# Decayed states in buffers of their own, and half of each row transfer asked for from ScalarE

## The chip, the cores and the metric

The kernel runs on one core of a Trainium2 chip. The core has five engines with an instruction queue each: TensorE (PE), VectorE (DVE), ScalarE (ACT), GpSimd (POOL) and SyncE (SP). Every queue is worked off in order; between engines, semaphores say when something is done. Data moves between the chip's memory and the core's buffers by DMA transfers, which an engine asks for with an instruction of its queue. The metric is the time of one execution on the device in microseconds (us); shorter is better. A change of less than about 1% is called no change here.

## What is computed

Stage 1 is a recurrent (mLSTM) layer over 4 batches, 8 heads, 768 steps and head dimension 40, stage 2 a mixture of 16 experts (4 groups of 4) over its 3072 output rows. Cut to what matters:

```python
for t in range(S):                                   # S = 768, per batch and head
    m_new = np.maximum(f_gate[:, :, t] + m, i_gate[:, :, t])
    f_stab, i_stab = np.exp(f_gate[:, :, t] + m - m_new), np.exp(i_gate[:, :, t] - m_new)
    C = f_stab * C + i_stab * outer(v_t, k_t)        # 40x40 state of each head
    n = f_stab * n + i_stab * k_t
    y[:, :, t] = sigmoid(o_gate[:, :, t]) * (C @ q_t) / max(|n . q_t|, 1)
# stage 2: x = y as [3072, 320]
g_idx = argmax(x @ w_group);  e_idx = argmax(x @ w_expert[g_idx])
out[row] = g_w * e_w * (relu(x[row] @ w1[g, e]) @ w2[g, e])   # w1 320x1024, w2 1024x320
```

## The kernel before

Stage 1 doesn't step through t. It cuts the 768 steps into 12 chunks of 64 and works on two batches at a time, so there are 24 units of work, called pairs here: pair u is chunk c = u // 2 of the batches 2p and 2p+1 with p = u % 2. Inside a chunk everything is a masked matrix product; from chunk to chunk a state `Cst[p]` (128x328, two of them, one for each p) is carried. The state of pair u is read and written again by pair u+2.

`unit(u)` issues the work of one pair. Up to pair 21 what it writes is the order on every engine; from pair 22 on a scheduler decides. In the order of the code, with the names that the rows show (`dst<-src`):

- SP asks for the rows of pair u+3: `load_qk` (L160, queries and keys, two transfers) and, further down, `load_nt` (L170, keys, values and gates, two transfers). There are four buffers of each.
- ACT: `gate_o`, the output gate's tanh (L165).
- PE: `carried(u)` (L239, `Y<-C,qk`): the queries against the state that was carried in; `state(u)` (L256, `Y<-nt,kw`): the chunk's own contribution to the state. Both write into parts of one tile, `Y`.
- POOL: `decayed(u)` (L263, `C<-C,decs`): the state times the chunk's decay, in place.
- DVE: `carried2(u)` (L245, `num<-Y,eacol`), then `state2(u)` (L270, `C<-C,Y`): adds the contribution. PE's `carried(u+1)` writes `Y` again, so it waits until `state2(u)` has read it.
- PE: `values(u)` (L281, `V<-nt,pt`), `scores(u+1)` (L214, `X<-qk`), one filler matmul `busy` (L141) and `decay(u+2)` (L180, L181, `aw`), which ACT turns into `ab` by 8 exponentials (L184).
- DVE: `norm(u)` (L291), `masked(u+1)` (L220, `pt<-X,ab`).
- POOL: `keyw(u+1)` (L227, `kw<-nt,ab`): the keys that `state(u+1)` reads; three buffers in turn.
- `turn(u-1)`: ACT copies, SP writes the pair's rows out (L323, `x_d<-x`), PE transposes them (L317, `tp`), ACT copies again (L333).
- DVE: denominators (`norm1`, L299 to L301) and `rows(u)` (L306, `xn`); POOL: `rows2(u)` (L311, `x<-xn,den`).
- POOL, from pair 6 on: `put_id` (L496, L497), which writes row numbers of the expert lists into the table `itab` in the chip's memory by an indirect DMA.

Every fourth pair, routing work of four earlier pairs is put between (`lg`, L349 to L450, on PE, DVE and ACT), and its weights `cb` are written behind the rows by SP (L452). From pair 12 on, weights of the first experts are asked for by SP (L608) and split into two parts by ACT (L650) and DVE (L652). Stage 2 starts by gathering expert rows: `ix<-itab`, `xg<-x_d,ix` (L590, POOL), a transposition `tpm` (L317, PE), and from there the expert matmuls (L767, L805 to L807).

Of the kernel before, what the change touches and what calls it, by code (L numbers as in the profile page):

```python
# [7 lines left out]
F32 = mybir.dt.float32  # L8
# [4 lines left out]
ALU = mybir.AluOpType  # L13
# [5 lines left out]
P = 128  # L19
B, H, S, D = 4, 8, 768, 40  # L20
L = 64
NP = B // 2
# [3 lines left out]
DM = H * D  # L26
# [9 lines left out]
D1 = D + 1  # L36
R4 = 4 * D1
NQK = 4
QR = 48
KR = 104  # L40
WIDE = 16
NAT = 976
K0, O0 = DM + H, 2 * DM + H
# [22 lines left out]
def bc(ap, shape):  # L66
    return ap.broadcast_to(list(shape))
# [3 lines left out]
def lstm_moe(ctx: ExitStack, tc: tile.TileContext, gates, qkT, nat, wcat, w1, w2, cst, out):  # L71
    nc = tc.nc
# [36 lines left out]
    def att_pool(name, bufs, **kw):  # L109
        return att.enter_context(tc.tile_pool(name=name, bufs=bufs, side="right", **kw))  # L110

    ap_ = att_pool("att", 1)
# [8 lines left out]
    mask_b = ap_.tile([P, L], BF16, name="mask_b")  # L121
    decs = ap_.tile([P, NCH, B * 4], F32, name="decs")
    Cst = [ap_.tile([P, 2, R4], F32, name=f"C{i}") for i in range(NP)]
    kws = [ap_.tile([P, DM + 24], F32, name=f"kw{i}") for i in range(3)]
    bcol = ap_.tile([P, NU, H], F32, name="bcol")
    eacol = ap_.tile([P, NU, H], F32, name="eacol")
    wk = att_pool("wk", 2)
# [9 lines left out]
    def busy(n):  # L137
        if n:
            t = ps_a.tile([P, 512], F32, name="busy", tag="aw", bufs=2)
        for _ in range(n):  # L140
            mm(t, ones_b, bc(ones_b.unsqueeze(1), (P, 4, P)), start=True, stop=True)  # L141
# [15 lines left out]
    def load_qk(u):  # L157
        qk = qkp[u % NQK]
        for r in range(2):
            nc.sync.dma_start(qk[64 * r:64 * r + QR, 4 * P * r:4 * P * r + 8 * P], qkT[u, r].rearrange("d i h t -> d (i h t)"))  # L160
        st_.setdefault(u, {})["qk"] = qk

    def gate_o(u):
# [3 lines left out]
    def load_nt(u):  # L167
        nt = ntp[u % NQK]
        for a in range(2):
            nc.sync.dma_start(nt[halves(a), K0 * a:K0 * a + NAT], nat[u, halves(a)])  # L170
        st_.setdefault(u, {})["nt"] = nt

    def halves(b):
        return slice(L * b, L * b + L)
# [42 lines left out]
    def masked(u):  # L217
        t = st_[u]
        pt = t["pt"] = wk.tile([P, 2, 4 * L], F32, name="pt")
        nc.vector.tensor_tensor(pt, X.rearrange("p r k t -> p r (k t)"), t["ab"].rearrange("p (r i) t -> p r (i t)", r=2),  # L220
                                op=ALU.mult)

    def keyw(u):
        t = st_[u]
        if u // NP < NCH - 1:
            kw = t["kw"] = kws[u % 3]
            nc.gpsimd.tensor_tensor(kw[:, 0:DM].rearrange("p (h d) -> p h d", d=D),  # L227
                                    t["nt"][:, K0:K0 + DM].rearrange("p (h d) -> p h d", d=D),
                                    bc(t["ab"][:, :, L - 1:L], (P, H, D)), op=ALU.mult)
# [29 lines left out]
    def decayed(u):  # L259
        c, p = divmod(u, NP)  # L260
        if 0 < c < NCH - 1:
            cb = Cst[p].rearrange("p a (i e) -> p (a i) e", e=D1)
            nc.gpsimd.tensor_tensor(cb, cb, bc(decs[:, c, p * 8:(p + 1) * 8].unsqueeze(2), (P, 8, D1)), op=ALU.mult)  # L263

    def state2(u):
        c, p = divmod(u, NP)
        if c < NCH - 1:
            st = Y[:, 0, R4:3 * R4].rearrange("p (a x) -> p a x", a=2)
            if c > 0:
                nc.vector.tensor_tensor(Cst[p], Cst[p], st, op=ALU.add)  # L270
            else:
                nc.vector.tensor_copy(Cst[p], st)

# [205 lines left out]
    def first_tokens():  # L479
        none = rt["rows"][0]  # L480
        t = itab[0:NE * NBLK].rearrange("(e n) p o -> e (n p o)", e=NE)
        n = 3 * P * WIDE // 2
        for k in range(2):
            nc.sync.dma_start(t[:, k * n:(k + 1) * n], none[0:NE, 0:n])
        nc.sync.dma_start(itab[NE * NBLK:NE * NBLK + 1].rearrange("a p o -> a (p o)"), none[0:1, 0:P * WIDE])

    def last_rows():
        zero = rt["rows"][1]
        for u in range(NU - 4, NU):
            nc.sync.dma_start(x_d[u * P:(u + 1) * P, :], zero)  # L490
        nc.sync.dma_start(x_d[NTOK:NTOK + 1, :], zero[0:1])
# [340 lines left out]
    def run(stage, u):  # L832
        if 0 <= u < NU:
            stage(u)
# [11 lines left out]

    def unit(u):
        run(load_qk, u + 3)
        if u == 6:
            first_tokens()  # L850
        if u == 9:
            last_rows()
        run(gate_o, u)
        with ExitStack() as st:
            if u == MANUAL:
                st.enter_context(tc.issue_after(rt["lg", u - 3].ins))
            run(carried, u)
        run(state, u)
        run(decayed, u)
        run(carried2, u)  # L860
        parts = ()
        if u % 4 == 1 and 1 < u < NU - 4:
            parts = [lambda f=f: f(u // 4 - 1, 4) for f in (logits_of, logits_at)]
        if u == NU - 4:
            parts = [lambda f=f: f(NG - 2, 3) for f in (logits_of, logits_at)]
        for f in parts[:1]:
            f()
        go_on()
        run(state2, u)
        run(values, u)  # L870
        run(scores, u + 1)
        busy(fill(u))
        run(decay, u + 2)
        run(norm, u)
        run(masked, u + 1)
        for f in parts[1:]:
            f()
        if u > NU - 4:
            run(logits, u - 2)
        if u == 9:  # L880
            chores.append(first_experts())
        if u == 21:
            chores.append(early_counts())
        run(keyw, u + 1)
        run(turn, u - 1)
        run(load_nt, u + 3)
        run(norm1, u)
        run(rows, u)
        run(rows2, u)
        if u == 5:  # L890
            first_rows()
        go_on(3)
        for _ in range(1 if u < 20 else 3):
            put_id()
# [57 lines left out]
    with tc.manual_schedule():  # L952
        nc.sync.dma_start(G[:, :, 0:P], gates[:, :, 0:P])
        nc.scalar.dma_start(cs, cst)
        nc.scalar.dma_start(G[:, :, P:], gates[:, :, P:])
        nc.vector.memset(ones_b, 1.0)
        nc.vector.memset(sep, 0.0)
        nc.scalar.activation(sep, sep, AF.Exp)
        busy(11)
        nc.vector.memset(R_, 1.0)  # L960
        nc.vector.memset(R_.rearrange("h (c t) -> h c t", t=L)[:, :, 0:1], 0.0)
        nc.vector.memset(Dl[:, 0:1], 0.0)
        nc.vector.memset(ohsum[0], 0.0)
        nc.vector.memset(Apc[96:P], 0.0)
        for t in kws:
            nc.gpsimd.memset(t[:, DM:], 0.0)
        for u in range(4):
            q = nc.vector if u % 2 == 0 else nc.gpsimd
            q.memset(qkp[u], 0.0)
            q.memset(ntp[u][0:64, V1:], 0.0)  # L970
            q.memset(ntp[u][64:P, 0:K0], 0.0)
            load_nt(u)
            load_qk(u)
        sel = cs[:, C_SELP:C_SELP + B * H].rearrange("q (a p i) -> q p i a", p=NP, a=2)
        for p in range(NP):
            nc.gpsimd.tensor_copy(selw[:, p].rearrange("q h (b t) -> q h b t", b=2), bc(sel[:, p].unsqueeze(3), (P, H, 2, L)))
        sums.append(gate_sums(0, P))
        nc.gpsimd.tensor_copy(id_b, ident)
        nc.gpsimd.tensor_copy(mask_b, cs[:, C_MASK:C_MASK + L])
        nc.gpsimd.tensor_copy(sel2_b, cs[:, C_SEL2:C_SEL2 + B * 4])  # L980
        nc.gpsimd.tensor_copy(par_b, cs[:, C_PAR:C_PAR + P])
        sum_on(7)
        scores(0)
        decay(0)
        keyw(0)
        sums.append(gate_sums(P, 2 * P))
        sum_on()
        masked(0)
        sum_on()
        decay(1)  # L990
        busy(9)
        state(0)
        values(0)
        scores(1)
        gate_o(0)
        keyw(1)
        norm(0)
        state2(0)
        masked(1)
        decay(2)  # L1000
        norm1(0)
        rows(0)
        rows2(0)
        sum_on()
        nc.gpsimd.iota(tokid[:, :, :, 0], pattern=[[P, NU], [0, WIDE // 2]], base=0, channel_multiplier=1)
        nc.gpsimd.tensor_copy(tokid[:, :, :, 1], bc(cs[:, C_TOK:C_TOK + NU].unsqueeze(2), (P, NU, WIDE // 2)))
        nc.vector.tensor_copy(keyb, cs[:, C_15E:C_15E + NE])
        nc.vector.tensor_copy(lt_b, cs[:, C_LT:C_LT + P])
        nc.vector.tensor_copy(base_b, cs[:, C_BASE:C_BASE + NE])
        nc.sync.dma_start(wc, wcat)  # L1010
        sum_on(7)
        sums.append(gate_sums(2 * P, S))
        for u in range(1, 5):
            unit(u)
            sum_on(2)
        sum_on(9)
# [96 lines left out]
    with tc.For_i(0, nv, 1):  # L1113
# [35 lines left out]
        h = hp.tile([P, NF, P], F32, name="hh")  # L1149
# [99 lines left out]
```

## Time and profile before

| what | value |
|---|---|
| median of 3 runs | 426.79 us (425.06 to 428.4) |
| the profiled execution, its own time | 427.83 us |
| its span in the profile | 426.2 us |
| mean granted TensorE clock | 0.921 |
| busy: PE | 373.5 us (88%) |
| busy: PE's weight loads (PEld) | 332.9 us (78%) |
| busy: DVE | 267.5 us (63%) |
| busy: ACT | 203.4 us (48%) |
| busy: POOL | 170.8 us (40%) |
| moved by DMA | 85.70 MB, 201 GB/s over the span |

The span reaches from the first to the last instruction that the profile holds; the time of the run is 1.6 us longer. Busy shares are means over two stages: stage 1 ends at about 188 us, stage 2 fills the rest. In the rows below, a line as L239 is a line of the kernel before, and `[2.03 <-DVE C L270]` says that the engine had been idle for 2.03 us before the instruction, and that DVE's write of C at line 270 released it.

### The profile page before, as it was taken

To read this page: it belongs to the slowest core of one execution; us is meant where nothing else is said; L and a number is where in the kernel's file an instruction comes from. 1 tells how busy PE (TensorE), PEld (TensorE's weight loads), DVE (VectorE), ACT (ScalarE), POOL (GpSimd) and SP (SyncE) were. 2 spreads that over 40 slices of the span, in tenths; PEclk is the share of its full clock that TensorE was granted. 3 is DMA by queue.
4 is the path that set the end of the run, shared out by engine and by line. 5 is a ranking of instruction groups with operands and counts; after the bars stand their busy time and mean duration, and the time that the engine had idled before them with its cause. 6 is when DMAs were issued, how large, how long until landed. Compare 5 with 4: busy or idle time off the path is not lost.

```text
span 426.2 us, 11056 instructions
## 1 busy us (share of the span) xinstructions
PE 373.5 (88%) x4205; PEld 332.9 (78%) x4205; DVE 267.5 (63%) x708; ACT 203.4 (48%) x560; POOL 170.8 (40%) x223
## 2 busy tenths in 40 slices
PE   5867696696778978799989999999999999999994
PEld 1456584575666766569979999999999999888993
DVE  7268454668687896557486667766657473555630
ACT  1326525164457443262385557557557652444630
POOL 7126624556666654324541312633331331423300
PEclk9989869699999875558999999999999999999998
DMA  8917638689899907664893236998653508878900
GB/s 188 212 27 186 145 86 197 156 244 251 234 260 270 226 9 175 205 196 103 319 359 156 59 97 256 398 377 318 232 205 124 183 24 287 287 266 299 392 25 10
DMA packets 29643, 85.70 MB, mean 201 GB/s; under 512 B 11895, under 2 KB 15981, under 8 KB 25971
## 3 DMA queue, kind: packets, MB, share of 16 engines
q1 hardware_dynamic: 24420, 67.95, 53.6%
q0 software_dynamic: 4944, 16.53, 11.3%
q8 instruction: 34, 0.56, 0.5%
q10 hardware_dynamic: 224, 0.49, 0.4%
q14 instruction: 21, 0.17, 0.1%
HBM read 74.80 MB, written 10.38 MB: 200 GB/s over the span
## 4 chain that ended last, share of the span: by engine, by line
PE 55%; DVE 13%; issue 11%; POOL 8%; DMA 8%; SPq 2%; ACT 1%; POOLq 1%; DVEq 0%; ACTq 0%
PE psh L767 13%; PE po L807 5%; PE po L805 5%; PE po L806 5%; DMA w2s<-in_w_dram 4%; PE psh L735 4%; PE X L214 3%; PE tpm L317 3%; POOL C L263 2%; PE V L281 2%; PE busy L141 2%; DMA nt<-in_nat_dram 2%; POOL itab L497 2%; DVE w2l L652 2%; PE po L781 2%
## 5 line engine op out<-in xcount | busy, mean ns | idle before, releaser
L594 POOL DMA_INDIRECT out_dram<-y,ix x32 | 35.4, 1105 | 89.2 <-ACT y L817 66.3
L184 ACT ACTIVATE ab<-aw,bcol 128x64 f32<-128x64 f32 x192 | 41.7, 332 | 59.7 <-PE aw L181 49.9
L805 PE MATMUL po<-w2h,hh 128*128 128x320 f32 (+3 forms) x200 | 63.3, 316 | 2.0 <-ACT hh L716 2.0
L807 PE MATMUL po<-w2h,hh 128*128 128x320 f32 (+3 forms) x200 | 62.1, 312 | 0.5 <-DVE hh L719 0.5
L806 PE MATMUL po<-w2l,hh 128*128 128x320 f32 (+3 forms) x200 | 61.7, 309 | 0.0
L652 DVE TENSOR_TENSOR w2l<-w2s,w2h 128x640 fp32r<-128x640 f32 x64 | 50.7, 825 | 16.3 <-ACT w2h L650 13.7
L590 POOL DMA_INDIRECT xg<-x_d,ix x32 | 34.2, 1069 | 48.1 <-DMA ix<-itab 27.7
L716 ACT ACTIVATE hh<-psh 128x256 fp32r<-128x256 f32 (+5 forms) x68 | 29.2, 430 | 39.2 <-PE psh L735 17.2
L650 ACT CAST w2h<-w2s 128x640 fp32r<-128x640 f32 x64 | 43.4, 724 | 5.7 <-DMA w2s<-in_w_dram 5.6
L735 PEld LDWEIGHTS psh<-xhl,w1s 128*128 128x128 f32 x336 | 40.9, 191 | 2.1 <-ACT y L817 2.1
L735 PE MATMUL psh<-xhl,w1s 128*128 128x144 f32 (+3 forms) x336 | 41.9, 284 | 0.0
L767 PE MATMUL psh<-xhl,w1h 128*128 128x256 f32 (+5 forms) x224 | 38.9, 297 | 0.7 <-ACT xhl L694 0.4
L239 PE MATMUL Y<-C,qk 40*64 40x41 f32 x704 | 16.9, 244 | 25.4 <-DVE C L270 25.4
L805 PEld LDWEIGHTS po<-w2h,hh 128*128 128x128 f32 (+3 forms) x200 | 36.4, 182 | 3.3 <-ACT hh L716 2.3
L239 PEld LDWEIGHTS Y<-C,qk 40*64 40x64 f32 x704 | 14.0, 149 | 30.5 <-DVE C L270 28.5
L807 PEld LDWEIGHTS po<-w2h,hh 128*128 128x128 f32 (+3 forms) x200 | 36.3, 182 | 1.7 <-DVE hh L719 1.5
L806 PEld LDWEIGHTS po<-w2l,hh 128*128 128x128 f32 (+3 forms) x200 | 36.5, 182 | 0.0
L311 POOL TENSOR_TENSOR x<-xn,den 128x320 f32<-128x320 f32 x20 | 15.8, 788 | 49.1 <-DVE xn L306 42.9
L497 POOL DMA_INDIRECT itab<-tokid,slot x24 | 25.5, 1063 | 23.8 <-DVE slot L428 8.8
L767 PEld LDWEIGHTS psh<-xhl,w1h 128*128 128x128 f32 x224 | 33.0, 199 | 1.4 <-ACT xhl L694 0.5
L817 ACT ACTIVATE y<-po,xg 128x320 f32<-128x320 f32 (+3 forms) x25 | 13.2, 527 | 43.6 <-PE po L807 38.4
L214 PE MATMUL X<-qk 104*64 104x128 f32 x384 | 30.9, 311 | 0.0
(212 smaller groups left out, 838.5 us busy)
## 6 DMA issues: line engine op xcount, KB each, us to landing
w1s<-in_w_dram SPq DMA_DIRECT2D x12, 1536.0 KB
w2s<-in_w_dram SPq DMA_DIRECT2D x12, 1280.0 KB
nt<-in_nat_dram SPq DMA_DIRECT2D x48, 244.0 KB
qk<-in_qkT_dram SPq DMA_DIRECT2D x48, 192.0 KB
x_d<-x SPq DMA_DIRECT2D x24, 192.0 KB
w1s<-in_w_dram SPq DMA_DIRECT2D x8, 384.0 KB
w1s<-in_w_dram POOLq DMA_DIRECT2D x2, 1536.0 KB
w2s<-in_w_dram SPq DMA_DIRECT2D x8, 320.0 KB
```

Source lines behind the costliest of these rows:

```text
L184: rt["exp"] = nc.scalar.activation(ab[:, i, :], aw[:, i, :], AF.Exp, bias=bcol[:, u, i:i + 1])
L214: mm(X[halves(a), :, 2 * b + m, :], qk[0:KR, k_cols(pr, b)], two(qk[0:KR, q_cols(0, pr, b)], Q1, L), start=True, stop=True)
L497: no_order("ids", nc.gpsimd.indirect_dma_start(out=itab_flat, out_offset=bass.IndirectOffsetOnAxis(ap=sl, axis=0), in_=tk, in_offset=None))
L590: return nc.gpsimd.indirect_dma_start(out=o, out_offset=None, in_=src, in_offset=bass.IndirectOffsetOnAxis(ap=idx, axis=0))
L594: return nc.gpsimd.indirect_dma_start(out=out, out_offset=bass.IndirectOffsetOnAxis(ap=idx, axis=0), in_=y, in_offset=None, bounds_check=N ...
L650: nc.scalar.copy(a, src[:, s])
L652: lows.append(lambda: nc.vector.tensor_tensor(o[rows], src[rows, s], a[rows].bitcast(F32), op=ALU.subtract))
L735: ins = mm(ps[:, g * W:(g + 1) * W], w1s[:, s], xhl[:, k, :], start=(k == 0), stop=(k == 2))
L767: ins = mm(ps[:, g * W:(g + 1) * W], w[:, s], x, start=(n == 0), stop=(n == len(todo) - 1))
L805: mm(po[0:m], hh[:, f, t], w2h[:, s], start=st0, stop=False)
L806: mm(po[0:m], hh[:, f, t], w2l[:, s], start=False, stop=False)
L807: ins = mm(po[0:m], hh[:, f, tl], w2h[:, s], start=False, stop=sp0)
```

## The change

Two things are changed.

First, the decayed state gets buffers of its own, `Cd[p]`. The decay is no longer made in place between `carried(u)` and `state2(u)`; `decayed(u+2)` is issued right behind `state2(u)`, from the state just summed, and `state2(u+2)` adds the pair's contribution to `Cd` into `Cst`. The decays of pair 2 are made in the start of the kernel, those of the others two pairs ahead. To make room, the buffers of `kw` go from three to two.

Second, of the two transfers of each `load_qk` and each `load_nt`, the second is asked for from ACT's queue instead of SP's: 48 requests in all, 8 of them in the start.

```diff
+    Cd = [ap_.tile([P, 2, R4], F32, name=f"Cd{i}") for i in range(NP)]
-    kws = [ap_.tile([P, DM + 24], F32, name=f"kw{i}") for i in range(3)]
+    kws = [ap_.tile([P, DM + 24], F32, name=f"kw{i}") for i in range(2)]
     def load_qk(u):
         for r in range(2):
-            nc.sync.dma_start(qk[64 * r:64 * r + QR, 4 * P * r:4 * P * r + 8 * P], qkT[u, r].rearrange("d i h t -> d (i h t)"))
+            (nc.scalar if r else nc.sync).dma_start(qk[64 * r:64 * r + QR, 4 * P * r:4 * P * r + 8 * P], qkT[u, r].rearrange("d i h t -> d (i h t)"))
     def load_nt(u):
         for a in range(2):
-            nc.sync.dma_start(nt[halves(a), K0 * a:K0 * a + NAT], nat[u, halves(a)])
+            (nc.scalar if a else nc.sync).dma_start(nt[halves(a), K0 * a:K0 * a + NAT], nat[u, halves(a)])
     def keyw(u):
-            kw = t["kw"] = kws[u % 3]
+            kw = t["kw"] = kws[u % 2]
     def decayed(u):
         if 0 < c < NCH - 1:
-            cb = Cst[p].rearrange("p a (i e) -> p (a i) e", e=D1)
-            nc.gpsimd.tensor_tensor(cb, cb, bc(decs[:, c, p * 8:(p + 1) * 8].unsqueeze(2), (P, 8, D1)), op=ALU.mult)
+            cb, cd = (t[p].rearrange("p a (i e) -> p (a i) e", e=D1) for t in (Cst, Cd))
+            nc.gpsimd.tensor_tensor(cd, cb, bc(decs[:, c, p * 8:(p + 1) * 8].unsqueeze(2), (P, 8, D1)), op=ALU.mult)
     def state2(u):
             if c > 0:
-                nc.vector.tensor_tensor(Cst[p], Cst[p], st, op=ALU.add)
+                nc.vector.tensor_tensor(Cst[p], Cd[p], st, op=ALU.add)
     def unit(u):
         run(state, u)
-        run(decayed, u)
         run(carried2, u)
...
         run(state2, u)
+        run(decayed, u + 2)
         run(values, u)
...
         state2(0)
+        decayed(2)
         masked(1)
```

Where this puts instructions is read from three queues. Names with numbers are buffers: C_103 and C_104 are the two states, Cd_105 and Cd_106 the new buffers, kw_105 to kw_108 the key weights, nt_92 to nt_95 and qk_88 to qk_91 the four buffers of the rows. Lines of the kernel after are one higher from L124 on.

POOL in the middle of stage 1, one pair and the beginning of the next, before:

```order
L497 DMA itab<-tokid,slot 49280x16
L263 TENSOR_TENSOR C_104<-C_104,decs 128x328
L227 TENSOR_TENSOR kw_106<-nt_94,ab 128x320
L311 TENSOR_TENSOR x<-xn,den 128x320
L496 MEMSET sep 1x1
L497 DMA itab<-tokid,slot 49280x16
L263 TENSOR_TENSOR C_103<-C_103,decs 128x328
L227 TENSOR_TENSOR kw_107<-nt_95,ab 128x320
```

The same place after:

```order
L498 DMA itab<-tokid,slot 49280x16
L264 TENSOR_TENSOR Cd_106<-C_104,decs 128x328
L228 TENSOR_TENSOR kw_107<-nt_94,ab 128x320
L312 TENSOR_TENSOR x<-xn,den 128x320
L497 MEMSET sep 1x1
L498 DMA itab<-tokid,slot 49280x16
L264 TENSOR_TENSOR Cd_105<-C_103,decs 128x328
L228 TENSOR_TENSOR kw_108<-nt_95,ab 128x320
```

The decay has the same place in the queue, between `put_id` and the next `kw`. Before, it is that of the pair at hand, waits for PE's `carried(u)` and is waited for by DVE's `state2(u)`; after, it is that of pair u+2, waits for DVE's `state2(u)` and is waited for two pairs later.

SP at the end of stage 1, from the rows of pair 22's queries on, before:

```order
L160 DMA qk_90<-in_qkT_dram 48x1024 x2
L323 DMA x_d<-x 128x384
L452 DMA x_d<-cb 128x3x8
L170 DMA nt_94<-in_nat_dram 64x976 x2
L608 ISA
L608 DMA w2s<-in_w_dram 128x640
L160 DMA qk_91<-in_qkT_dram 48x1024 x2
L452 DMA x_d<-cb 128x4x8
L323 DMA x_d<-x 128x384
L452 DMA x_d<-cb 128x8
L170 DMA nt_95<-in_nat_dram 64x976 x2
```

The same place after:

```order
L161 DMA qk_90<-in_qkT_dram 48x1024
L324 DMA x_d<-x 128x384
L171 DMA nt_94<-in_nat_dram 64x976
L609 ISA
L609 DMA w2s<-in_w_dram 128x640
L161 DMA qk_91<-in_qkT_dram 48x1024
L453 DMA x_d<-cb 128x4x8
L324 DMA x_d<-x 128x384
L171 DMA nt_95<-in_nat_dram 64x976
```

The last two loads of `nt` (pairs 22 and 23) no longer stand behind the writes of `cb` 128x3x8 and 128x8, and half of each load is gone from the queue.

ACT in one pair in the middle of stage 1, before:

```order
L650 CAST w1h<-w1s 128x1024
L165 ACTIVATE nt_93<-nt_93 128x320
L364 COPY lT<-lg 128x128
L184 ACTIVATE ab<-aw,bcol 128x64 x8
L322 COPY x<-x 128x64
L333 COPY xT<-tp 128x384
```

The same place after:

```order
L171 DMA nt_95<-in_nat_dram 64x976
L651 CAST w1h<-w1s 128x1024
L161 DMA qk_88<-in_qkT_dram 48x1024
L166 ACTIVATE nt_93<-nt_93 128x320
L365 COPY lT<-lg 128x128
L185 ACTIVATE ab<-aw,bcol 128x64 x8
L323 COPY x<-x 128x64
L334 COPY xT<-tp 128x384
L171 DMA nt_92<-in_nat_dram 64x976
```

ACT now asks for a half of `qk` ahead of the pair's tanh and exponentials, and for a half of `nt` behind its copies.

## Rows read from the trace of the kernel before

**Rows 1.** Waits of PE, in 30 to 82, 82 to 135 and 135 to 190 us.

```profile
PE Y L239 <- DVE C L270: 13.9, 5, 7.0
...
PE Y L239 <- DVE C L270: 8.7, 8, 2.0
...
PE Y L239 <- DVE C L270: 2.7, 2, 2.2
```

**Rows 2.** Waits of DVE, 82 to 135 us (us in total, times, longest).

```profile
DVE C L270 <- POOL C L263: 11.3, 9, 2.5
```

**Rows 3.** Chain that ended last, 105 to 130 us (start us, us, what).

```profile
120.90 0.76 POOL C L263
...
125.08 1.01 POOL itab L497
...
126.12 0.76 POOL C L263
```

**Rows 4.** Timeline, one pair (start us, us, engine, line, form, [idle before <-releaser]).

```profile
116.26 0.74 POOL L227 TENSOR_TENSOR kw<-nt,ab 128x320 f32<-128x320 f32 x1
...
117.16 0.68 DVE L220 TENSOR_TENSOR pt<-X,ab 128x512 f32<-128x512 f32 x1
...
117.50 0.79 PE L256 MATMUL Y<-nt,kw 128*64 128x82 f32 x16
...
118.68 1.04 PE L214 MATMUL X<-qk 104*64 104x128 f32 x16
...
118.84 0.72 POOL L311 TENSOR_TENSOR x<-xn,den 128x320 f32<-128x320 f32 x1 [1.84 <-DVE xn L306]
```

**Rows 5.** Timeline of PE, the carried part of two pairs in a row.

```profile
99.96 0.68 PE L239 MATMUL Y<-C,qk 40*64 40x41 f32 x32 [2.03 <-DVE C L270]
...
105.19 0.68 PE L239 MATMUL Y<-C,qk 40*64 40x41 f32 x32 [1.29 <-DVE C L270]
```

**Rows 6.** Stretches: us; busy of PE, PEld, DVE, ACT, POOL; granted clock; DMA share; GB/s.

```profile
82.00:107.00 25.00, 21.08 (x503) 17.45 (x503) 19.67 (x68) 13.56 (x57) 14.47 (x23) 1.00 0.79 214
...
107.00:135.00 28.00, 22.73 (x544) 18.95 (x534) 20.23 (x67) 14.51 (x58) 16.46 (x26) 1.00 1.00 254
...
158.00:189.00 31.00, 25.49 (x202) 19.55 (x201) 17.71 (x91) 11.16 (x29) 10.97 (x17) 0.50 0.67 179
```

**Rows 7.** Timeline, POOL, first write of row numbers (itab).

```profile
75.74 1.17 POOL L497 DMA_INDIRECT itab<-tokid,slot  x1 [5.69 <-DMA nt<-in_nat_dram]
```

**Rows 8.** Timeline, POOL and PE at 44 us.

```profile
43.84 0.73 POOL L227 TENSOR_TENSOR kw<-nt,ab 128x320 f32<-128x320 f32 x1
...
44.45 1.05 PE L239 MATMUL Y<-C,qk 40*64 40x41 f32 x32 [2.86 <-DVE C L270]
```

**Rows 9.** Timeline, last loads of the start and first decays.

```profile
12.83 1.16 SPq L160 DMA_DIRECT2D qk<-in_qkT_dram  x2
...
14.56 3.38 ACT L184 ACTIVATE ab<-aw,bcol 128x64 f32<-128x64 f32 x16 [2.58 <-PE aw L181]
```

**Rows 10.** Timeline of SP, two halves asked for in a row.

```profile
138.82 2.12 SPq L170 DMA_DIRECT2D nt<-in_nat_dram  x2
```

**Rows 11.** Timeline from 158 us on, last loads and first expert rows.

```profile
158.64 1.11 SPq L170 DMA_DIRECT2D nt<-in_nat_dram  x2
...
163.47 1.36 PE L281 MATMUL V<-nt,pt 128*64 128x82 f32 x16 [1.05 <-DMA nt<-in_nat_dram]
...
166.61 0.20 PE L408 MATMUL lg<-oh,lt_b 128*128 128x16 bf16 x1
...
177.69 1.00 POOL L590 DMA_INDIRECT xg<-x_d,ix  x1 [3.70 <-DMA ix<-itab]
...
178.99 0.95 POOL L590 DMA_INDIRECT xg<-x_d,ix  x1 [0.30 <-issue]
...
182.15 0.90 PE L317 MATMUL tpm<-cs,xg 128*128 128x128 f32 x3
...
186.76 0.90 PE L317 MATMUL tpm<-cs,xg 128*128 128x128 f32 x3
```

## Prediction

> **What bounds the kernel now.** I read the page first: PE is busy for 373.5 of 426.2 us, so only its idle time can be won, and most of that lies in stage 1. Then the waits of PE by stretch. One kind of wait stands out, PE's `carried` part (L239) waiting for DVE's state sum (L270): 13.9 us in 30 to 82 us, 8.7 us in 82 to 135 us and 2.7 us behind that [rows 1], 25.3 us in all. The waits of DVE say what the sum itself waits for: POOL's in-place decay, 11.3 us in the middle stretch alone [rows 2]. The chain of waits shows the turn that this makes: a decay at 120.90, the next at 126.12, 5.22 us apart, with the 1.01 us of `put_id` right ahead of the second [rows 3]. POOL comes to the decay late, because it stands behind the row product `x` and the table write of the pair before. PE alone would need less: `carried` starts at 99.96 and at 105.19, and the second had waited for 1.29 us, so PE's own work for a pair is 105.19 − 1.29 − 99.96 = 3.94 us [rows 5].
>
> The transfers are the second limit. In 82 to 107 us the DMA engines are busy for 0.79 of the time, in 107 to 135 us, where weights come on top of the rows, for all of it [rows 6].
>
> **The change part by part. The decay.** The product itself costs what it cost, 0.76 us on POOL in the same place of the queue [rows 3] and as often; that of pair 2 in the start lies on a POOL that has time there, and I cost it at nothing. What is gained is its place in the chain: `state2(u)` finds `Cd` ready since two pairs ago, so DVE sums at once and PE's `carried(u+1)` goes on. What is late next is `kw`: it still stands on POOL behind table write and decay, and `state(u+1)` waits for it. I follow that loop in [rows 4]: end of `kw` 117.00 to `state` 117.50, 0.50; to the start of X at 118.68, 1.18; X 1.04; from `pt` at 117.16 to `x` at 118.84 (DVE makes `xn` behind the next pair's `pt`), 1.68; from `x` at 118.84 to the next decay at 120.90 [rows 3], 2.06, then the decay 0.76 and `kw` 0.74. Together 7.96 us, but the loop spans two pairs: 3.98 us for one, about PE's own 3.94. So neither POOL nor the loop keeps PE from its own pace, and the middle could win all 8.7 us, were it for the engines alone.
>
> From 30 to 82 us: 7.0 of the 13.9 us are one wait [rows 1], at the first table write, which POOL starts at 75.74 after 5.69 us of waiting [rows 7]. That stays, and now holds up `kw(8)` instead of the decay of pair 7. Before, decay, sum and `carried` (0.68 [rows 5]) follow it ahead of `state(8)`; after, decay and `kw`. Between 0 and 2 us are won; I take 1.2, since DVE has by then done `pt` and `xn` of the pair that it could not reach before. Of the other 6.9 us, at 44 us `kw` ends at 44.57 and `carried` ran from 44.45 to 45.50 [rows 8]: `state` can come forward by 0.93 us of the 2.86 us waited, a third. A third of 6.9 is 2.3; the upper end is all 6.9. Sum −3.5, bounds 0 and −8.9.
>
> From 82 to 135 us: the waits are spread over the stretch; by its length 25/53 of 8.7 = 4.1 us fall in 82 to 107 us, where DMA has 0.21 × 25 = 5.2 us free, and 4.6 us in 107 to 135 us, where it has none [rows 1, 6]. A faster PE asks for rows sooner and gets them no sooner there. I take 3.5 and 0.5: −4.0, bounds 0 and −8.7.
>
> Two buffers of `kw`: `kw(u+1)` now waits for `state(u−1)` instead of `state(u−2)`; by [rows 4] `state` is done well over one pair before that. Nothing; it would cost if POOL ran more than a pair ahead, which the loop above excludes.
>
> **The requests.** SP gives off 48 requests at 1.11/2 = 0.56 us [rows 11], hidden on SP, which mostly waits. ACT takes two for each pair, 1.1 us. It is busy for 14.51 of 28 us in its fullest stretch [rows 6], 2.75 of 5.3 us for a pair, so 3.9 of the new 4 to 5 us: it fits, if the requests themselves don't wait. They can: on SP two in a row took 2.12 instead of 1.11 us once, 1.0 for an earlier transfer to land [rows 10]. In the start, SP's last two requests go out from 12.83 to 13.99, and ACT's first decays begin at 14.56 after an idle 2.58 us [rows 9]; if ACT's requests were as late, 0.3 to 0.6 us of cover is left for two small exponentials. I take +0.2 for all of it, bounds 0 and +8 (ACT late in each of the eight fullest pairs by 1 us).
>
> The Trainium skill speaks against the halves, in "DMA: Bandwidth & Descriptors", section "Rules for kernel authors": two transfers to disjoint partition halves share the same 16 DMA engines even when two engines ask for them, and spreading requests saves only issue time. By that rule the second part of the change brings no bandwidth, as the sum above has it too; the trace agrees as far as it goes, with a DMA share of 1.00 in 107 to 135 us [rows 6].
>
> **The end of stage 1.** SP asks for `nt` of pair 22 at 158.64 only, behind a write of `cb`, and V of that pair waits 1.05 us for it at 163.47 [rows 11]. In SP's new order both last loads stand ahead of that, and the last X, `carried` and V come earlier in PE's. What stage 2 starts on is a chain: the routing matmul at 166.61, gathers at 177.69 and 178.99, the first transposition 182.15, 4.46 us behind its gather; the second one could be at 178.99 + 4.46 = 183.45, but PE reaches it at 186.76, having the last pair in front of it [rows 11]. These 3.3 us can go; the routing matmul moves behind more of pair 23 and may come 0.5 to 1 us later. I take −2.5, bounds −3.3 and +1. The clock counts here: TensorE has 0.50 of its clock in 158 to 189 us, that is 1.2 GHz, against 1.00 in 82 to 135 us, 2.4 GHz [rows 6]; I leave it as it is.
>
> **Sum** for the profiled execution: 427.83 − 3.5 − 4.0 − 2.5 + 0.2 = 418.0 us. It lay 427.83 − 426.79 = 1.04 us over the median, so I say 417.0 us.
>
> **The rivals.**
> R1, transfers bound the middle, and the end is pinned by the gathers. For it: share 1.00 and rows that land just in time. Against: 82 to 107 us has room. Only the −3.5 stays: 427.83 − 3.5 − 1.04 = 423.3 us.
> R2, all waits go but the 7.0 us one: 6.9 + 8.7 + 2.7 = 18.3, so 427.83 − 18.3 − 1.04 = 408.5 us. For it: the loop of 3.98 us. Against: the DMA share, and `kw` behind the same work on POOL.
> R3, the change moves the wait and no more: PE waits for `kw` instead of the sum. The turn of 5.22 us stays, if the loop spans one pair rather than two, that is, if `x` of a pair waits for X of the next but one to be masked. Then 424 to 427 us, by whether the end wins its 2.5.
> R4, ACT becomes the bound, slower than before. Requests in an in-order queue hold up the exponentials behind them. Per pair 2.75 + 1.1 + 2 × 1.0 = 5.9 us if each request waits as in [rows 10]. It decides from a wait of 0.7 us each on (2.75 + 1.1 + 1.4 = 5.25, the present turn). At 5.9, ten pairs are 0.6 to 0.7 us longer, +6.5, and the middle wins nothing: 427.83 + 6.5 − 2.5 − 1.04 = 430.8 us, up to 434 without the end's gain. For it: share 1.00, where transfers land late. Against: the request for `qk` is made three pairs ahead, and half the waiting stays on SP.
>
> **How the numbers follow.** Forecast 0.43 (412 to 422 us by its bounds, taken together), R1 0.19, R2 0.13, R3 0.11, R4 0.14. The range leaves out R4's upper part and the lower part of R2: 409 to 427 us. About 1% is what a measurement of this kernel can tell from no change: faster is below 422.5, slower above 431.1. Faster: 0.43 + 0.13 and two fifths of R1, 0.64. Slower: two thirds of R4, 0.09. The same: 0.27.
>
> **What would show it.** Right: PE's wait at `carried` for the state sum all but gone; decays on POOL about 4.3 us apart in 82 to 107 us and still near 5 in 107 to 135 us; the 7 us wait at the first table write now at `state`; `nt` of pair 22 asked for before 150 us; the second `tpm` within 2 us of the first. R3 would show the same 5.2 us turn with PE waiting at `state` for `kw`, R4 PE waiting at `aw`'s readers, with ACT idle in front of a request. Wrong would make it a clock that falls further because PE pauses elsewhere, or a scheduler's order at the end in which the routing matmul waits for the last `nt`.

## The result

The changed kernel takes 417.9 us (median; 411.84 to 421.1) where the kernel before takes 426.95 us in the same comparison: ratio 0.969, interval 0.959 to 0.979. A second comparison gave 417.42 against 426.56 us, ratio 0.982, interval 0.973 to 0.991. So the change is worth 2 to 3%, some 8 to 13 us; 417.0 us were forecast. Single executions of one kernel here lie up to 9 us apart, and the granted clock goes with them; the ratios leave disturbed executions out.

The profiled execution took 415.53 us, with a span of 413.9 us and a clock of 0.93. Its waits of PE, in 30 to 82, 82 to 135 and 135 to 190 us (waiter <- releaser: us in total, times, longest), answer to [rows 1]:

```profile
PE Y L257 <- POOL kw L228: 8.8, 4, 5.5
...
PE Y L240 <- DVE C L271: 0.6, 1, 0.6
...
PE Y L257 <- POOL kw L228: 4.7, 3, 2.1
...
PE Y L240 <- DVE C L271: 1.1, 2, 0.6
...
PE Y L257 <- POOL kw L228: 0.8, 1, 0.8
```

PE's wait at `carried` (now L240) for the state sum is down from 13.9 to 0.6 us in the first stretch and from 8.7 to 1.1 us in the second. In its place PE waits at `state` (L257) for `kw`: 8.8 and 4.7 us. That is what the prediction named as late next. In the first stretch it is less waiting than the prediction left over (13.9 − 3.5 = 10.4 us); in the second it is as much as the prediction left over (8.7 − 4.0 = 4.7 us), but the prediction had put that down to the transfers. The stretches, with the columns of [rows 6]:

```profile
82.00:107.00 25.00, 20.80 (x496) 17.37 (x494) 22.62 (x78) 14.10 (x59) 15.44 (x24) 1.00 1.03 235
...
107.00:135.00 28.00, 24.27 (x489) 19.61 (x489) 20.16 (x60) 14.90 (x51) 15.70 (x24) 0.88 1.05 251
...
158.00:189.00 31.00, 25.30 (x147) 22.04 (x148) 22.21 (x91) 10.89 (x20) 13.76 (x15) 0.67 0.34 93
```

The DMA engines are now busy all the time from 82 to 135 us, and PE is less busy in 82 to 107 us than before (20.80 against 21.08 us). In 107 to 135 us TensorE was granted 0.88 of its clock, where the kernel before had 1.00 [rows 6]. So the middle, where 4 us were to be won, doesn't look like the place of the gain. To see where it is I read from PE's timeline when the values matmuls (V) of four pairs begin and when the first expert matmul does, for the kernel before, for two executions of the kernel after, and for the experiments below:

| kernel | V of pair 0 at | V 0 to V 8 | V 8 to V 17 | V 17 to V 23 | V 23 to first expert matmul | from there to the span's end |
|---|---|---|---|---|---|---|
| before | 21.1 | 59.3 | 49.2 | 46.7 | 11.9 | 238.0 |
| after | 19.0 | 52.2 | 50.6 | 34.8 | 19.2 | 238.1 |
| after, second execution | 21.3 | 52.2 | 49.6 | 38.3 | 19.1 | 238.7 |
| decay alone | 20.6 | 55.2 | 45.5 | 43.2 | 13.7 | 240.0 |
| requests alone | 19.0 | 57.2 | 49.7 | 33.9 | 17.7 | 237.6 |
| after, table later | 21.4 | 49.5 | 50.8 | 37.7 | 19.2 | 235.7 |
| after, thin rows | 19.0 | 51.9 | 45.0 | 31.5 | 18.5 | |
| before, thin rows | 21.2 | 57.6 | 48.7 | 39.4 | 14.9 | |
| decay alone, thin rows | 21.1 | 54.0 | 45.6 | 36.2 | 14.9 | |
| after, requests not in the middle | 19.0 | 51.2 | 47.0 | 37.0 | 17.3 | 238.4 |
| the same, table later | 21.0 | 46.5 | 46.6 | 37.1 | 17.0 | 236.8 |
| the same, kw ahead of the decay | 20.9 | 48.5 | 45.9 | 38.5 | 16.6 | 235.0 |

(With thin rows the routing comes out otherwise, so stage 2 of those three is not compared.) Of the 12.3 us between the two profiled executions, 2.1 lie in the start, 7.1 between pair 0 and pair 8, −1.4 between 8 and 17, and 4.6 from there to the first expert matmul; stage 2 takes the same time. Not all of this is the change's: the granted clock differs by stretch and by execution, as the experiments show.

### The profile page after: what moved, and what is told of

It reads as the page before. It is cut to its first block, busy times and chain, and to the rows that moved or that the text cites. A ratio compares the mean times of both kernels' runs of the same rounds, so it can differ in the third digit from the quotient of the medians.

```text
span 413.9 us, 11061 instructions
## 1 busy us (share of the span) xinstructions
PE 364.9 (88%) x4205; PEld 325.3 (79%) x4205; DVE 268.1 (65%) x708; ACT 203.2 (49%) x560; POOL 172.5 (42%) x222
## 4 chain that ended last, share of the span: by engine, by line
PE 48%; DMA 21%; DVE 11%; issue 10%; ACT 4%; POOL 3%; POOLq 1%; SPq 1%; ACTq 0%; DVEq 0%
PE psh L768 13%; DMA nt<-in_nat_dram 10%; DMA w2s<-in_w_dram 7%; PE po L808 5%; PE po L806 5%; PE po L807 5%; PE psh L736 3%; PE X L215 2%; PE tpm L318 2%; DMA ix<-itab 2%; PE V L282 2%; ACT ab L185 2%; DVE w2l L653 2%; DMA wc<-in_wcat_dram 1%; PE Y L257 1%
## 5 line engine op out<-in xcount | busy, mean ns | idle before, releaser
L653 DVE TENSOR_TENSOR w2l<-w2s,w2h 128x640 fp32r<-128x640 f32 x64 | 50.8, 827 | 19.4 <-ACT w2h L651 19.3
L591 POOL DMA_INDIRECT xg<-x_d,ix x32 | 35.8, 1118 | 51.0 <-DMA ix<-itab 19.5
L768 PE MATMUL psh<-xhl,w1h 128*128 128x256 f32 (+5 forms) x224 | 37.8, 292 | 0.2 <-DVE hh L720 0.2
L498 POOL DMA_INDIRECT itab<-tokid,slot x24 | 27.0, 1126 | 25.2 <-DVE slot L429 16.0
L257 PE MATMUL Y<-nt,kw 128*64 128x82 f32 x352 | 18.9, 254 | 15.5 <-POOL kw L228 14.3
L768 PEld LDWEIGHTS psh<-xhl,w1h 128*128 128x128 f32 x224 | 32.1, 194 | 0.6 <-PE psh L768 0.5
L257 PEld LDWEIGHTS Y<-nt,kw 128*64 128x64 f32 x352 | 15.2, 147 | 18.9 <-POOL kw L228 16.7
L215 PE MATMUL X<-qk 104*64 104x128 f32 x384 | 29.8, 304 | 0.2
L725 DVE SCALAR_TENSOR_TENSOR hh<-psh,hh 128x256 fp32r<-128x256 f32 (+5 forms) x44 | 19.3, 462 | 13.1 <-ACT hh L717 12.7
```

Of the source, the lines that this page charges most:

```text
L215: mm(X[halves(a), :, 2 * b + m, :], qk[0:KR, k_cols(pr, b)], two(qk[0:KR, q_cols(0, pr, b)], Q1, L), start=True, stop=True)
L257: mm(two(Y[64 * r:64 * r + 64, 0, o:o + D1], R4, D1), t["kw"][:, i * D:i * D + 64], v_both(u, i), start=True, stop=True)
L591: return nc.gpsimd.indirect_dma_start(out=o, out_offset=None, in_=src, in_offset=bass.IndirectOffsetOnAxis(ap=idx, axis=0))
L653: lows.append(lambda: nc.vector.tensor_tensor(o[rows], src[rows, s], a[rows].bitcast(F32), op=ALU.subtract))
L768: ins = mm(ps[:, g * W:(g + 1) * W], w[:, s], x, start=(n == 0), stop=(n == len(todo) - 1))
```

## The experiments

### The two parts apart, and the change again

*Decay alone*: the kernel after with every request back on SyncE.

```diff
-            (nc.scalar if r else nc.sync).dma_start(qk[...
+            nc.sync.dma_start(qk[...
-            (nc.scalar if a else nc.sync).dma_start(nt[...
+            nc.sync.dma_start(nt[...
```

> The kernel after with all loads of rows asked for from SyncE again: the decay part alone. Theory A (the decay wins the early pairs, the requests win the end): V of pair 8 starts 6 to 9 us earlier than before (80.4), PE's wait at carried for the state sum is gone as in the kernel after, but SP still stands at the write of cb ahead of the rows of pair 22, and the end of stage 1 loses what was won or keeps only part: 420 to 424 us, ratio 0.984 to 0.994. Theory B (the decay is the whole change, the end follows by itself): 415 to 419 us, ratio 0.97 to 0.982.

*Requests alone*: the kernel before with the two lines of the change in `load_qk` and `load_nt`.

> The kernel before with the second half of each load of rows asked for from ScalarE: the requests alone. Theory A: PE still waits about 20 us or more at carried for the state sum up to 135 us, V of pair 8 starts at 78 to 81 us, but the rows of pair 22 are asked for before 155 us and the first expert matmul comes 3 to 7 us earlier than 188.2: 419 to 424 us, ratio 0.98 to 0.993. Theory B: no change within 1%, 425 to 429 us. If the first state matmul starts at 18.3 instead of 20.3 us here and not with the decay alone, the requests win the 2 us of the start; if it goes either way in both, it is the clock.

*The changed kernel again.*

> The changed kernel itself, for more times and a second profile. Theory A: 414 to 420 us, ratio 0.965 to 0.985, V of pair 8 at 71 to 73 us, of pair 22 at 151 to 155 us. The state matmul of pair 0 at 18.3 again would say that the 2 us of the start belong to the change; at 20.3 that they are the clock's.

Measured: decay alone 418.21 us (ratio 0.978, 0.973 to 0.984, ten runs); requests alone 419.05 us (0.987, 0.975 to 1.0); both 417.42 us (0.982, 0.973 to 0.991). The three intervals overlap: by itself each part is worth, as far as these times tell, nearly what both together are, so the parts don't add up. The time alone would have pointed to theory B for the decay, and pair 8 came 4.6 us earlier than before, not the 6 to 9 of theory A. With the requests alone pair 8 came at 76.2 us and the first expert matmul 10.7 us earlier than before, both sooner than theory A had them. With both again, pair 8 came at 73.5 and pair 22 at 155.3 us, just behind the ranges. The table shows the parts by stage. The decay alone gains 4.1 us up to pair 8 and 3.7 us from there to pair 17; the requests gain 2.1 us up to pair 8, lose 0.5 in the middle, and bring V of pair 23 forward by 12.8 us. Put together, the middle is 4.1 to 5.1 us slower than with the decay alone.

The waits of PE with the decay alone, in 30 to 82 and in 82 to 135 us, show the same exchange of `carried` for `kw` as the whole change:

```profile
PE Y L257 <- POOL kw L228: 10.9, 5, 7.0
...
PE Y L257 <- POOL kw L228: 4.8, 6, 1.4
```

With the requests alone PE still waits for the state sum, in the same two stretches:

```profile
PE Y L239 <- DVE C L270: 11.7, 5, 4.8
...
PE Y L239 <- DVE C L270: 3.9, 4, 1.4
```

11.7 and 3.9 us where before had 13.9 and 8.7: theory A's "20 us or more" was too much, 15.6 us are left. In the middle nothing was won by it, V of pair 17 comes 49.7 us behind V of pair 8, before 49.2; there the waiting has only moved.

What the requests win up to pair 8 is less than the table makes it look. In the kernel after, SP comes to the first filling of the table `itab` at

```profile
58.84 3.40 SPq L485 DMA_DIRECT2D itab<-w1s  x2
```

and with the decay alone, where SP asks for all the halves itself, 4.55 us later:

```profile
63.39 0.84 SPq L485 DMA_DIRECT2D itab<-w1s  x2
```

`put_id` waits for that filling, as a row of the second execution of the kernel after shows,

```profile
69.70 1.16 POOL L498 DMA_INDIRECT itab<-tokid,slot  x1 [5.20 <-DMA itab<-w1s]
```

and PE waits for POOL: 5.5 us at longest after, 7.0 us with the decay alone. But 1.7 of the 4.55 us lie ahead of V of pair 0 (19.0 and 20.6 us), and another 1.7 between V of pair 4 and V of pair 6, which took 13.9 us after and 15.6 us with the decay alone. There the granted clock differed: in 50 to 62 us it was 1.00 after, 0.86 with the decay alone and 0.72 before. After (the clock stands in front of the DMA share),

```profile
50.00:62.00 12.00, 11.06 (x269) 9.56 (x267) 9.23 (x27) 6.12 (x26) 7.48 (x10) 1.00 0.62 147
```

and in *table later*, a version below whose code is that of the kernel after up to pair 6,

```profile
50.00:62.00 12.00, 11.79 (x213) 10.06 (x215) 4.82 (x15) 3.78 (x18) 3.31 (x6) 0.72 0.26 65
```

That version took 16.9 us from V of pair 4 to V of pair 6, as the kernel before did. So the 3.0 us that the kernel after is faster there can't be credited to the change, and some 1.1 of the 4.55 us are left for the halves taken from SP (0.3 us by the second execution).

The kernels with thin rows, below, are second executions of this stretch, since they differ only from the loads of pair 12 on: from V of pair 0 to V of pair 8 the decay alone takes 54.0 us there instead of 55.2, with 5.8 us instead of 7.0 as the longest wait for `kw`, and before takes 57.6 us instead of 59.3. The 2.1 us that the requests seem to win up to pair 8 are therefore not shown to be theirs. What is clear of this scatter is the decay from V of pair 0 to V of pair 4: 25.5 us in all three executions without it, 22.4 to 23.4 us in all nine with it.

The start: V of pair 0 begins at 19.0 or at about 21 us, and the same program did both. The nine filler matmuls ahead of it in the first profile of the changed kernel,

```profile
16.30 2.10 PE L142 MATMUL busy<-ones_b 128*128 128x512 bf16 x9 [1.08 <-ACT ab L185]
```

and in the second,

```profile
16.31 4.00 PE L142 MATMUL busy<-ones_b 128*128 128x512 bf16 x9 [0.98 <-ACT ab L185]
```

The granted clock in 14 to 20 us was 0.92 there and 0.50 here (the column in front of the DMA share). First profile:

```profile
14.00:20.00 6.00, 4.92 (x62) 3.01 (x61) 1.52 (x4) 3.96 (x19) 1.48 (x2) 0.92 1.05 221
```

second:

```profile
14.00:20.00 6.00, 5.02 (x20) 1.75 (x17) 1.26 (x3) 3.92 (x19) 1.47 (x2) 0.50 1.05 225
```

So the 2.1 us of the start are the clock's, not the change's; decay alone had the slower, requests alone the faster one.

### What binds the middle

In the three thin kernels only a quarter of the columns of `nt` is loaded from pair 12 on; requests, places and order stay.

```diff
     def load_nt(u):
         nt = ntp[u % NQK]
+        w = NAT if u < 12 else NAT // 4
         for a in range(2):
-            (nc.scalar if a else nc.sync).dma_start(nt[halves(a), K0 * a:K0 * a + NAT], nat[u, halves(a)])
+            (nc.scalar if a else nc.sync).dma_start(nt[halves(a), K0 * a:K0 * a + w], nat[u, halves(a), 0:w])
```

> The changed kernel with a quarter of the columns of nt loaded from pair 12 on (both halves keep their requests and places; the rest of the buffer keeps older values, so this part of the computation is left out): 366 KB of about 1.4 MB a pair less. From V of pair 8 to V of pair 17 the changed kernel took 49.6 and 50.6 us in two executions. Theory A (the transfers bound the middle, by their bytes): 41 to 46 us here. Theory B (the engines' turn binds, or ScalarE's queue holds regardless of bytes): 48 to 51 us.

> The kernel before with the same cut of nt from pair 12 on (that part of the computation is left out). From V of pair 8 to V of pair 17 before took 49.2 us. If the turn of 5.2 us through the decay on POOL binds it, 47 to 49.5 us here, whatever the bytes; if the transfers bound it too, 41 to 46 us.

> The decay part alone (all requests on SyncE) with a quarter of the columns of nt from pair 12 on (that part of the computation is left out). With full rows V of pair 17 came 45.5 us behind V of pair 8, with PE waiting 4.8 us for kw. If bytes hold it there: 40 to 43 us. If the engines' loop through kw does: 44.5 to 46 us, with the wait for kw still there.

From V of pair 8 to V of pair 17 the kernel before takes 48.7 us with thin rows and 49.2 with full ones: its turn through the in-place decay binds it, whatever the bytes, and PE still waits there (82 to 135 us; lines of the thin kernels are one higher):

```profile
PE Y L240 <- DVE C L271: 7.2, 7, 1.4
```

The decay alone takes 45.6 us with thin rows and 45.5 with full ones: bytes don't bind it either. What PE waits for most is `kw`, 5.2 us where full rows had 4.8:

```profile
PE Y L258 <- POOL kw L229: 5.2, 7, 0.8
```

Only the whole change feels the bytes: 45.0 us thin, 49.6 and 50.6 full. Both waits of PE are alike there (5.2 us for `kw` with thin rows), so the difference doesn't lie in them. Most of it lies late, from V of pair 13 to V of pair 17: 23.2 and 22.5 us in the kernel after and 22.5 with the requests alone, but 19.0 with thin rows and 19.7 with the decay alone. ACT's waits tell what differs. In the kernel after, 82 to 160 us, ACT stands ahead of the tanh (L166) for transfers:

```profile
ACT nt L166 <- DMA nt<-in_nat_dram: 12.4, 3, 5.8
...
ACT nt L166 <- DMA w2s<-in_w_dram: 4.1, 2, 2.7
...
ACT nt L166 <- DMA x_d<-cb: 3.8, 1, 3.8
```

20.3 us in these three rows. The longest of them, 5.8 us, is another matter:

```profile
147.04 0.47 ACT L166 ACTIVATE nt<-nt 128x320 f32<-128x320 f32 x1 [5.79 <-DMA nt<-in_nat_dram]
```

ACT's timeline has no request in these 5.79 us; this tanh waits for its own rows, those of pair 22, asked for at 137.54 and 139.49 us. The other 14.5 us stand behind requests, 10.4 of them ahead of V of pair 17. With thin rows no wait of ACT that the profile puts down to a transfer is over 1.1 us, this one is 0.7:

```profile
ACT nt L166 <- DMA w2s<-in_w_dram: 0.7, 1, 0.7
```

and with the decay alone ACT waits for PE instead, as it should:

```profile
ACT ab L185 <- PE aw L182: 14.8, 8, 3.1
...
ACT nt L166 <- DMA nt<-in_nat_dram: 0.6, 1, 0.6
```

What ACT waits for in the 14.5 us are not its own operands. One pair in the kernel after (timeline; a queue's name with q is a request):

```profile
114.55 0.47 ACTq L171 DMA_DIRECT2D nt<-in_nat_dram  x1
...
116.12 0.32 ACTq L161 DMA_DIRECT2D qk<-in_qkT_dram  x1
...
116.49 0.47 ACT L166 ACTIVATE nt<-nt 128x320 f32<-128x320 f32 x1 [3.87 <-DMA nt<-in_nat_dram]
...
117.81 1.08 POOL L228 TENSOR_TENSOR kw<-nt,ab 128x320 f32<-128x320 f32 x1 [2.40 <-DMA nt<-in_nat_dram]
```

ACT makes two requests ahead of the tanh, which each wait for an earlier transfer to land; the tanh starts after 3.87 us of this, right behind the second request, and the exponentials come behind it. Its own rows had landed long before: POOL's `kw` of that pair, which reads them, began at 111.97 us. POOL's `kw` meanwhile waits 2.40 us for `nt`, whose half was asked for late in the same way. With the DMA engines busy all the time (1.05 in 107 to 135 us), a request costs ACT the landing of others, and the pair's exponentials stand behind it.

Part of the loss is the clock. Of the 5.1 and 4.1 us by which the two executions of the kernel after are slower than the decay alone from V of pair 8 to V of pair 17, 2.0 and 1.2 lie between V of pair 16 and V of pair 17, where the granted clock fell to 0.50; in the first, PE had just waited 1.76 us for `kw`. With the decay alone it stayed at 1.00 in 107 to 135 us. In the first execution:

```profile
114.00:120.00 6.00, 5.80 (x74) 4.15 (x70) 2.64 (x9) 2.24 (x11) 3.33 (x6) 0.50 1.04 248
```

Whether it would have fallen without ACT's waits is not shown. The other 3.1 and 2.8 us come ahead of it.

The Trainium skill, in "DMA: Bandwidth & Descriptors", section "Rules for kernel authors", says that spreading requests over engines gives no bandwidth and saves issue time only. The traces agree: 251 GB/s in 107 to 135 us after, 254 before [rows 6], 265 with the requests alone and 251 with the decay alone. The issue time saved on SP is what is left of the 4.55 us ahead of the table's filling, some 1.1 us; the same requests cost ACT more where transfers were late.

### The requests out of the middle, and the table later

*Requests not in the middle*: the halves of pairs 10 to 20 go back to SyncE.

```diff
-            (nc.scalar if r else nc.sync).dma_start(qk[...
+            (nc.scalar if r and not 9 < u < 21 else nc.sync).dma_start(qk[...
-            (nc.scalar if a else nc.sync).dma_start(nt[...
+            (nc.scalar if a and not 9 < u < 21 else nc.sync).dma_start(nt[...
```

> The changed kernel with the halves of pairs 10 to 20 asked for from SyncE, those of the start and of the last three pairs from ScalarE as in the change. V of pair 8 should come 52 us behind V of pair 0, as in the changed kernel. Theory A (bytes bind the middle): V of pair 17 is 100 to 102 us behind V of pair 0, as in all kernels with the decay so far, and the time is that of the changed kernel within 2 us. Theory C (the requests in ScalarE's queue cost the middle 4 to 5 us, since from pair 8 to 17 the decay alone took 45.5 and the whole change 50 us): 96 to 99 us, and 412 to 415 us.

Measured: 410.83 us, ratio 0.968 (0.965 to 0.971). Pair 17 comes 98.2 us behind pair 0, 47.0 us behind pair 8: theory C, with a time 1 us below its range. The requests in ACT's queue cost the middle some 3 us against this version, and the bytes are the same in both. From V of pair 13 to V of pair 17 it takes 19.4 us, as the decay alone does. ACT's waits for transfers ahead of the tanh, 20.3 us in 82 to 160 us with the requests, are down to one, behind the last request:

```profile
ACT nt L166 <- DMA nt<-in_nat_dram: 2.5, 1, 2.5
```

*Table later*: the kernel after, with no write of row numbers in pairs 6 and 7 and two each in pairs 8 and 9.

```diff
-        for _ in range(1 if u < 20 else 3):
+        for _ in range(0 if u < 8 else 2 if u < 10 else 1 if u < 20 else 3):
             put_id()
```

> The changed kernel with the first writes of row numbers held back by two pairs (none in pairs 6 and 7, two in pairs 8 and 9). The wait of POOL for the table's first filling (5.5 us of PE waiting for kw at about 70 us) should go. Theory A (the middle is bound by transfers): V of pair 8 comes 4 to 5 us earlier, V of pair 17 less than 2 us earlier, the time moves by less than 2 us from the changed kernel's. Theory B (engines bind the middle): all of 4 to 5 us reaches the end, 412 to 414 us.

Measured: 413.16 us (0.972, 0.963 to 0.981), 4 us under the changed kernel's 417.42 beside it. In 30 to 82 us PE's longest wait for `kw` falls from 5.5 to 2.9 us, though there are more of them:

```profile
PE Y L257 <- POOL kw L228: 8.2, 6, 2.9
```

Pair 8 comes 2.7 us earlier, less than either theory said, and pair 17 about 2 us; the time is theory B's. From V of pair 4 to V of pair 6, ahead of the edit, this execution had lost 3.0 us at the lower clock (0.72 in 50 to 62 us), so the edit itself may be worth more up to pair 8. Its stage 2 was 2.4 us shorter in the profiled execution, which nothing here explains; so how much of the 4 us the table is stays open.

*Both together.*

> As the one with the requests of pairs 10 to 20 on SyncE, and the first table writes two pairs later (the version that should be the fastest of all). Theory A: V of pair 17 still 99 to 102 us behind V of pair 0, 412 to 415 us. Theory C: 94 to 98 us, 408 to 412 us.

Measured: 407.76 us, ratio 0.962 (0.956 to 0.967), the lowest of all: 93.1 us from pair 0 to pair 17, on theory C's side, though 0.9 us below its range.

*kw ahead of the decay*: in that version, POOL's order within a pair is turned round.

```diff
         run(state2, u)
-        run(decayed, u + 2)
...
         run(keyw, u + 1)
+        run(decayed, u + 2)
```

> The fastest version so far (requests of pairs 10 to 20 on SyncE, table writes two pairs later) with kw of the next pair ahead of the decay of pair u+2 on POOL. If what PE still waits for in the middle is kw behind the decay (4.7 us in 82 to 135 us there), that wait falls below 2.5 us, V of pair 17 comes 2 to 4 us earlier than 46.6 us behind V of pair 8, and the time is 404 to 407 us. If the transfers hold the middle, the wait moves to loads and the time stays within 1.5 us of 407.8.

Measured: 407.82 us, ratio 0.965 (0.951 to 0.978), no change from 407.76. PE's waits in 82 to 135 us, without the edit:

```profile
PE Y L257 <- POOL kw L228: 4.7, 7, 0.9
...
PE X L215 <- DMA qk<-in_qkT_dram: 3.4, 1, 3.4
...
PE Y L240 <- DVE C L271: 0.5, 1, 0.5
```

and with it:

```profile
PE X L215 <- DMA qk<-in_qkT_dram: 4.7, 1, 4.7
...
PE Y L257 <- POOL kw L228: 2.6, 6, 0.7
...
PE Y L240 <- DVE C L271: 1.5, 2, 0.9
```

The wait for `kw` falls by 2.1 us, nearly as expected (2.6 us, not below 2.5), but the sum gets 1.0 us later and a load of `qk` 1.3 us later. The middle is 0.7 us shorter, not 2 to 4, and nothing of it is seen in the time. V of pair 8 came 2.0 us later behind V of pair 0 than without the edit, in an execution with a clock of 0.72 in 50 to 62 us against 1.00, so a gain of 1 or 2 us would not have shown. Here the waits have no single owner left.

## Why the prediction was right or wrong

**What binds before: right.** The kernel before keeps its pace with a quarter of the bytes (48.7 us), so the turn through the in-place decay bound it, as read from the chain of waits [rows 3].

**30 to 82 us: −3.5 forecast, −7.1 measured.** Of the 7.1 us, 3.0 lie between V of pair 4 and V of pair 6 and go with the granted clock (1.00 against 0.72), which the prediction left as it was. The change's own share is nearer the forecast: 2.2 us from V of pair 0 to V of pair 4, where every kernel with the decay is 2 us or more ahead, and 1.9 us from pair 6 to pair 8, around the first table write, where the kernel before itself differs by 1.8 us between the full and the thin execution. That the requests, which I had given no gain here, add to it by the earlier filling of the table is not shown beyond some 1 us.

**82 to 135 us: −4.0 forecast, +1.4 and +0.4 measured** in the two executions. The number was right for the decay alone, −3.7, but its reason was wrong: I cut 8.7 to 4.0 for the transfers, and the thin rows show that bytes take nothing from the decay. The place was wrong too: I gave 3.5 us to 82 to 107 us, where the DMA engines had room, and 0.5 to the rest; the decay alone won 1.0 us from V of pair 8 to V of pair 13 and 2.6 from there to V of pair 17 (0.1 and 3.1 us by the thin kernels). What keeps the rest is `kw`: 4.8 us of waits stay at `state`. My loop of 3.98 us left no such wait; it was worked out from one pair's rows with nothing late. The decays on POOL, which should have been 4.3 us apart in 82 to 107 us, were 5.2 us apart there on the mean in the kernel after and 5.5 us with the decay alone. The wait that the rival R3 named came for about half of the time.

**Requests: +0.2 forecast, 4.1 to 5.1 us lost in the middle.** This is the step that failed: the term for ACT's requests was 0.2 us, and against the decay alone they went with a loss of 4.1 to 5.1 us, of which 1.2 to 2.0 us came with a lower clock. The bound, 8 us, held it, and the mechanism was rival R4's: requests wait for landings in an in-order queue with the exponentials behind them. I let one row of a 1.0 us longer pair of requests [rows 10] pass for the exception, since it stood on SP, where nothing showed what it cost. In the start the same step was right: ACT's last request ended at 13.89 us, in the cover I had read from [rows 9].

**End: −2.5 forecast, −4.6 and −1.2 measured** from pair 17 to the first expert matmul. Right in kind. In the kernel after, SP asks for `nt` of pairs 22 and 23 at 139.49 and 149.74, and PE comes to the last V sooner; the timeline, with the routing matmul, the gathers and the transpositions:

```profile
139.49 0.47 SPq L171 DMA_DIRECT2D nt<-in_nat_dram  x1
...
149.74 0.65 SPq L171 DMA_DIRECT2D nt<-in_nat_dram  x1
...
151.59 0.79 PE L282 MATMUL V<-nt,pt 128*64 128x82 f32 x16
...
156.91 0.18 PE L409 MATMUL lg<-oh,lt_b 128*128 128x16 bf16 x1
...
166.94 1.00 POOL L591 DMA_INDIRECT xg<-x_d,ix  x1 [1.75 <-DMA ix<-itab]
...
168.25 0.95 POOL L591 DMA_INDIRECT xg<-x_d,ix  x1 [0.30 <-issue]
...
172.48 1.54 PE L318 MATMUL tpm<-cs,xg 128*128 128x128 f32 x6
```

Both `tpm` stand side by side at 172.48; before, 4.6 us lay between them [rows 11]. With the decay alone SP still stands at the write of `cb`, asks for the two loads at 148.57 and 157.51, and the two `tpm` are again 4.6 us apart:

```profile
148.57 1.11 SPq L171 DMA_DIRECT2D nt<-in_nat_dram  x2
...
157.51 1.12 SPq L171 DMA_DIRECT2D nt<-in_nat_dram  x2
...
167.71 1.00 POOL L591 DMA_INDIRECT xg<-x_d,ix  x1 [3.24 <-DMA ix<-itab]
...
172.06 0.90 PE L318 MATMUL tpm<-cs,xg 128*128 128x128 f32 x3 [1.50 <-DMA xg<-x_d,ix]
...
176.68 0.90 PE L318 MATMUL tpm<-cs,xg 128*128 128x128 f32 x3
```

But the gathers follow the routing matmul by 10.0 us (156.91 to 166.94) as before by 11.1, and that matmul stood behind more of pair 23, as forecast. So V of pair 23 came forward by 8 to 12 us against pair 17, and 7 of these went to waiting for the gathers (19.2 us from V of pair 23 to the first expert matmul, before 11.9). The clock has a part here as well: from V of pair 17 to V of pair 23 it was 0.72 on the mean before, 0.90 and 0.82 after. Between the two executions of the kernel after this part differs by 3.4 us; the size can't be given closer.

**The sum** came out because terms erred against each other, in the first and the second execution: up to pair 8 by −3.6 us in both, in the middle by +5.4 and +4.4, at the end by −2.1 and +1.3, and the clock of the start by −2.1 in the first only. That they cancelled was luck: what binds the kernel before was read rightly, the time was met, and the distribution over the stages was wrong.

## What to carry to other kernels

When a wait on a busy queue is removed, ask what else stands behind the same work: here waits for `kw` came in place of more than half of the waits for the sum. A DMA request was not a cheap instruction on an engine that computes: while transfers landed late it waited for others, and held everything behind it; give it to an engine with nothing behind it, or to one that computes only where transfers land early. Time two parts of a change apart before crediting either: here each alone was worth about what both were, and taking one of them out of one stretch gave 410.83 us, where the whole change gave 417.9 and 417.42. And before a stretch's difference is credited to an edit, look at its granted clock, and at a second execution of the same code: here 3.0 us up to pair 8 were the clock's.

## What was not expected of the hardware

The same program got 0.92 of TensorE's clock in one execution and 0.50 in another over the same 6 us of the start (14 to 20 us), with nine fillers at 2.10 or at 4.00 us: the 2.4 and the 1.2 GHz level. That is 2 us of the span that no edit made. The same holds for 50 to 62 us, 1.00 or 0.72 with the same code up to pair 6. And two requests held ACT for the most part of 3.87 us while the DMA engines were at a share of 1.05; with thin rows, at 0.84, waits of that kind were nearly gone (0.7 us at most ahead of the tanh). The kernel after with thin rows, 107 to 135 us:

```profile
107.00:135.00 28.00, 23.80 (x541) 19.22 (x537) 25.93 (x69) 19.09 (x69) 19.74 (x29) 1.00 0.84 225
```
